# Late attention blocks: values two visits after their scores, an own buffer for transposed blocks, exponentials summed by ScalarE, and TensorE's order left free for longer

## The chip, the cores and the metric

The kernel runs on one core of one Trainium2 chip. The metric is the device time of one execution in microseconds (us); less is better. Before the change it took 1091.05 us, the median of three runs (1088.34, 1091.05 and 1091.76).

A core has several engines that run at the same time, each through its own fixed list of instructions: TensorE (PE in the profile; PEld is its loading of weights), VectorE (DVE), ScalarE (ACT), GpSimd (POOL) and SyncE (SP). SP and POOL here mostly issue DMA transfers, each from a queue of its own and in order. An instruction that must wait holds up everything behind it on its engine.

## The reference

Attention inside blocks of 64 tokens, and behind it a feed-forward layer with PReLU. Cut to what is computed:

```python
# q, k, v: (8, 8, 576, 64) float32; 9 chunks of 64 tokens in each (batch, head)
scores = (1 / sqrt(64)) * q_c @ k_c.transpose
scores = scores - max(scores, axis=-1, keepdims=True)
attn = exp(scores)
attn = attn / (sum(attn, axis=-1, keepdims=True) + 1e-09)
x = (attn @ v_c) laid out as 4608 tokens x 512

h = x @ w_in                              # 512 x 2048
g = maximum(h, 0) + alpha * minimum(h, 0)
out = g @ w_out                           # 2048 x 512
```

## The kernel before

**Tiling.** The 4608 tokens are 36 subtiles of 128 tokens (two chunks of 64, eight heads), and 9 blocks of 512 tokens (four subtiles). The width of 2048 is cut into 16 slices `f` of 128. Every matrix product of the feed-forward layer is done three times, with a high and a low part of each operand in float32r (high x high, high x low, low x high); `split_weight` (L119 to L138) makes the two parts of the weights on ScalarE and VectorE, 32 times, one tile `wi` and one tile `wo` for each `f`.

**Plain stage.** Blocks 0, 1 and 2 are multiplied as they stand. A step is one (block, `f`): `ffn_in` (L314 to L334; 12 matmuls of 128x512 in L320, then PReLU and the split of its result into `gh` and `gl`), and later `ffn_out` (L336 to L347; 12 matmuls in L344, which add to four banks `ps_o0` to `ps_o3`). There are 48 steps, n = 0 to 47, in five phases: block 0 with f 0 to 3, block 1 with f 0 to 8, block 0 with f 4 to 15, block 1 with f 9 to 15, block 2. The four banks serve one phase at a time: at its end `store` (L351 to L380) empties them. The first part of blocks 0 and 1 goes to DRAM, and at the end of the block's second phase it is read back and added on VectorE (L367) in a tile of the name `raw` or `t1`. The first matmul of the next phase's `ffn_out` into a bank waits until that bank has been read. The second half of a step follows its first half one step later while n < 4, and two steps later from there on (the list `pending`).

**Paired stage.** Blocks 3 to 8 go in three pairs, each by a scheme with seven products in place of eight. Each of the seven weights is a sum or difference of quarters of the weights. `combine(side, j)` (L478 to L507) makes them, 16 times: 8 VectorE operations, two ScalarE copies, two tiles `t1` (two buffers), two tiles `raw` (three buffers), and seven DMAs on POOL that write the results to DRAM (`keep_a`). They come back through SP's queue as a stream (L524) through five buffers. `first_product(j)` (L591 to L622, matmuls in L586), eight times in a pair, computes h and PReLU; `second_product` (L624 to L697, matmuls in L669) the rest. For it `operand` builds the seven operands: for operand 7 a difference on VectorE in a tile `t3` with one buffer (L633), another difference in place (L636), then `split` on ScalarE and VectorE (L542, L543). Every third operand splits into the two `t1` tiles, the others into `gh` and `gl`. `convert` (L545 to L569) does the same for x of the next pair, between.

**Attention.** Subtiles 0 to 7 are done early, with buffers of their own. Subtiles 8 to 35 are done in **visits** (L399 to L413). A visit takes two banks `ps_a` and does the values of an old subtile (32 matmuls of 64x64, L283) and the scores of a new one (32 matmuls, L196) on TensorE, then copies the old result into x (`attn_x`), does the softmax of the new one (`attn_softmax`: maxima L210, subtraction L216, one exponential over 128x512 on ScalarE L217, sums L226, reciprocal, scaling L229), and `attn_blocks`: VectorE transposes 32x32 blocks (L236) into a tile taken from the one buffer named `q_sb`, and eight DMAs on SP's queue (L243) move those blocks to `pT`, which the values read. The old subtile is always the one before the new. The loads of the next subtile (q into that same `q_sb`, k, v; L156, L158, L165) are called after the visit. Subtiles 8 to 20 are visited at the plain steps 23, 25, 27, 29, 31, 33, 34, 36, 37, 39, 40, 42, 43; the others ahead of each `first_product` of the first and second pair. The last pair has no visits.

**What sets the order.** A scheduler orders each engine's instructions by dependences, buffers and priorities; attention work, PReLU and the emptying of banks have high priority. TensorE's matmuls are kept in the order of the program from step 4 on (`pinned`, L710; `pe`, near L107). Combines come at every odd step from 15 on, one each.

Of the kernel before, what the change touches and what calls it, by code (L numbers as in the profile page):

```python
# [27 lines left out]
def tile_local_attention_prelu_ffn(  # L28
# [12 lines left out]
    nc = tc.nc  # L41
# [15 lines left out]
    JF = NF // 2  # L57
    EARLY = 2 * SPB

    BIASED = (6,) * SPB + (8,) * SPB  # L60
    TURNS = (4, 9)
    HIGH = 300

# [141 lines left out]
    def attn_softmax(s, sc3):  # L205
        early = s < EARLY
        mx = soft.tile([P, H, 1], F32, name="mx", bufs=2)
        parts = [(slice(0, H), sc3)] if early else [(slice(b * NP, (b + 1) * NP), sc3[b]) for b in range(2)]
        for g, part in parts:
            nc.vector.tensor_reduce(mx[:, g], part, axis=AX.X, op=ALU.max)  # L210
        pr = prs[s // 2 % 2][:, s % 2] if early else soft.tile([P, H, C], F32, name="pr")
        sm = soft.tile([P, H, 1], F32, name="sm", bufs=2)
        m = BIASED[s] if early else 0
        if not early:
            for g, part in parts:
                nc.vector.tensor_tensor(pr[:, g], part, mx[:, g].broadcast_to([P, NP, C]), op=ALU.subtract)  # L216
            nc.scalar.activation(pr, pr, AF.Exp, scale=SCALE)  # L217
        elif m < H:
            nc.vector.tensor_tensor(pr[:, m:], sc3[:, m:], mx[:, m:].broadcast_to([P, H - m, C]), op=ALU.subtract)
            nc.scalar.activation(pr[:, m:], pr[:, m:], AF.Exp, scale=SCALE)  # L220
        if m:
            nc.vector.tensor_scalar(mx[:, :m], mx[:, :m], -SCALE, None, op0=ALU.mult)
            for g in range(m):
                nc.scalar.activation(pr[:, g], sc3[:, g], AF.Exp, bias=mx[:, g], scale=SCALE, accum_out=sm[:, g])
        if m < H:
            nc.vector.tensor_reduce(sm[:, m:], pr[:, m:], axis=AX.X, op=ALU.add)  # L226
        nc.vector.tensor_scalar(sm, sm, 1e-9, None, op0=ALU.add)
        nc.vector.reciprocal(sm, sm)
        nc.vector.tensor_tensor(pr, pr, sm.broadcast_to([P, H, C]), op=ALU.mult)  # L229
        probs[s] = pr  # L230

    def attn_blocks(s):

        pr = probs.pop(s)
        tb = load.tile([P, 2, H, HALF], F32, name="q_sb")
        nc.vector.transpose(tb.rearrange("p j h t -> p h j t"), pr)  # L236
        pT = load.tile([P, 2, H, HALF], F32, name="pT")
        for c in range(2):
            for i in range(2):
                for j in range(2):  # L240
                    src = slice(c * C + i * HALF, c * C + (i + 1) * HALF)
                    dst = slice(c * C + j * HALF, c * C + (j + 1) * HALF)
                    nc.sync.dma_start(  # L243
                        out=pT[dst, i].rearrange("p h t -> p (h t)"),
                        in_=tb[src, j].rearrange("p h t -> p (h t)"),
                    )
        pdiag[s] = pT
# [151 lines left out]
    def visit(old, new):  # L399

        att[:] = [ps_a.tile([P, TB], F32, name="ps_a") for _ in range(2)]
        with tc.high_priority(offset=HIGH):
            if old is not None:
                xo = attn_values(old)
            if new is not None:
                sc3 = attn_scores(new)
            if old is not None:
                attn_x(old, xo)
            if new is not None:
                attn_softmax(new, sc3)  # L410
                attn_blocks(new)
        if new is not None and new + 1 < NSUB:
            attn_load(new + 1)  # L413

    attn_load(0, "q")
    fetch("wi", 0)
# [23 lines left out]
            if 0 <= i - st < SPB:  # L440
                beside[i * n0 // (SPB + 2)].append((st, SPB + i - st))

    visits = [2 * NF - 9 + 2 * j for j in range(SPB + 1)]
    visits += [2 * NF + 1 + 3 * j // 2 for j in range(2 * SPB)]
    late = {}
    for j, at in enumerate(visits):
        old, new = EARLY + j - 1, EARLY + j
        late[at] = (old if j else None, new)

    pending = []  # L450

# [172 lines left out]
    def second_product(g, b, conversion, end):  # L624
# [4 lines left out]
        def operand(i, j):  # L629
            b11, b12, b21, b22 = g[j][:, 0], g[j][:, 1], g[JF + j][:, 0], g[JF + j][:, 1]  # L630
            if i == 7:
                t = stage.tile([P, TB], F32, name="t3", bufs=1)
                nc.vector.tensor_tensor(t, b22, b12, op=ALU.subtract)  # L633
            elif i in (5, 6, 4):
                one, two = {5: (b12, b11), 6: (b22, b12), 4: (b21, b12)}[i]
# [1 line left out]
                t = b12  # L637
            else:
                t = {1: b11, 3: b22, 2: b21}[i]
            pool, names = (stage, ("t1", "t1")) if count[0] % 3 == 2 else (gp, ("gh", "gl"))  # L640
            count[0] += 1
            hi, lo = (pool.tile([P, TB], F32R, name=name) for name in names)
            split(t, hi, lo)
# [61 lines left out]
    for n, (p, b, f) in enumerate(steps):  # L705
# [4 lines left out]
                x[b + 1] = new_x()  # L710
        if n == 2 * NF:
            new_raw(PLAIN)
        pinned[0] = n >= n0
        for st, s in beside[n]:
            attend(st, s)
        if n in late:
            if late[n][0] is None:
                attn_load(late[n][1])
            visit(*late[n])
        if ready < NF:  # L720
            prepare(ready)
            ready += 1
        elif n % 2 and combined:
            combine(*combined.pop(0))
        if n == len(steps) - 3:
            ops, conversion = convert(PLAIN)
# [3 lines left out]
                    conversion.pop(0)()  # L730
        pending.append((acc, ffn_in(x[b], f), f, f0, f1, b, False))

        if len(pending) > (1 if n < n0 else 2):
            second(*pending.pop(0))
    assert not combined and not conversion
    for _ in range(3):
# [6 lines left out]
    for pair in range(NPAIR):  # L743
# [5 lines left out]
        for j in range(JF):  # L749
            if more:  # L750
                new += 1
                visit(new - 1, new if new < NSUB else None)
            first_product(ops, g, j)
        if more:
            ops, conversion = convert(b + 2)
# [40 lines left out]
```

## Time and profile before

| | value |
|---|---|
| median of 3 runs | 1091.05 us |
| the profiled execution's own time | 1095.3 us |
| its span, first to last instruction | 1093.5 us |
| TensorE busy, matmuls / weight loads | 893.8 us (82%) / 695.3 us |
| VectorE busy | 745.1 us (68%) |
| ScalarE busy | 494.6 us (45%) |
| GpSimd busy | 115.5 us (11%) |
| mean granted TensorE clock | 0.897 |
| moved by DMA | 184.51 MB, 169 GB/s |
| chain that ended last, shares | PE 50%, DVE 18%, DMA 16%, SP's queue 7%, waiting for nothing shown 5%, ACT 3% |

How to read the rows: engines are PE, PEld, DVE, ACT, POOL, SP; a name with q is that engine's DMA queue. `L320` is line 320 of the kernel. `out<-in` names the tiles, `x24` counts. A row of the waits gives the waiting engine, tile and line, then what released it, the summed wait in us, how often, and the mean. A row of the timeline gives the start in us from the span's start, the duration, engine, line, operation and, in brackets, the idle time before it with its releaser. A row of the page's 40 slices has one digit for each slice of 27.3 us: the busy share, or the granted clock, in tenths.

### The profile page before, as it was taken

Reading aid. Unit: us, or ns where it says so; the run is one execution under the profiler, and the core shown is the slowest. Engines: PE = TensorE matmul, PEld = TensorE weight load, DVE = VectorE, ACT = ScalarE, POOL = GpSimd, SP = SyncE. Lnnn points to the kernel's source line nnn. Section 1 sums busy time; section 2 is a strip of 40 time slices with the busy share of each in tenths; the row PEclk is TensorE's granted clock in tenths of the full one; section 3 lists DMA queues with packets and bytes.
Section 4 is the critical chain, followed back from the end, with each engine's and each line's share of the span. In section 5 each row is a group of like instructions: output and inputs, shape, how many; then the busy total and the mean of one; then the engine's idle time right before and its main releaser. Section 6 shows DMA issues by size and latency. Waiting matters only on the chain.

```text
span 1093.5 us, 14954 instructions
## 1 busy us (share of the span) xinstructions
PE 893.8 (82%) x5248; PEld 695.3 (64%) x5248; DVE 745.1 (68%) x1369; ACT 494.6 (45%) x946; POOL 115.5 (11%) x174
## 2 busy tenths in 40 slices
PE   4889999766755688967685899787786999998998
PEld 3568887545544567756563577665664778886676
DVE  6799998865684346545457876555559784657875
ACT  6666565423232234433345454334355543665543
POOL 4023232423042000000000001000000001000000
PEclk9889999887876888978888899988897999999999
DMA  9557673565456221454545357645442567554464
GB/s 281 171 182 245 213 255 128 193 196 175 136 186 213 65 59 51 145 164 142 165 146 165 96 192 217 217 131 196 129 160 86 165 193 250 193 183 163 154 194 153
DMA packets 69211, 184.51 MB, mean 169 GB/s; under 512 B 11408, under 2 KB 18576, under 8 KB 69136
## 3 DMA queue, kind: packets, MB, share of 16 engines
q1 hardware_dynamic: 56672, 143.17, 42.1%
q0 software_dynamic: 12320, 40.38, 10.2%
q8 instruction: 42, 0.69, 0.3%
q14 instruction: 33, 0.27, 0.1%
q10 hardware_dynamic: 144, 0.01, 0.0%
HBM read 135.27 MB, written 40.89 MB: 161 GB/s over the span
## 4 chain that ended last, share of the span: by engine, by line
PE 50%; DVE 18%; DMA 16%; SPq 7%; issue 5%; ACT 3%; POOL 0%; DVEq 0%; ACTq 0%; POOLq 0%
PE ps_o L669 12%; PE ps_o L586 9%; PE ps_h L320 8%; DMA q_sb<-qT 8%; PE ps_o L344 8%; SPq L243 7%; PE ps_h L669 6%; PE ps_h L586 4%; DMA pT<-q_sb 3%; PE ps_a L196 2%; DMA wi<-kT 2%; DVE t L633 1%; DMA wo_a<-raw 1%; DVE q_sb L236 1%; DVE gl L543 1%
## 5 line engine op out<-in xcount | busy, mean ns | idle before, releaser
L344 PE MATMUL ps_o<-wo,gh 128*128 128x512 f32 x384 | 119.7, 395 | 1.4 <-DVE raw L367 1.4
L320 PE MATMUL ps_h<-xh,wi 128*128 128x512 f32 x384 | 119.1, 437 | 0.8 <-ACT xh L301 0.8
L586 PE MATMUL ps_o<-wi,raw 128*128 128x512 f32 x222 | 96.1, 433 | 0.0
L196 PE MATMUL ps_a<-k_sb,q_sb 64*64 64x64 f32 x896 | 28.7, 295 | 82.1 <-DMA q_sb<-qT 82.1
L210 DVE TENSOR_REDUCE mx<-ps_a 128x4 f32<-128x256 f32 (+1 forms) x64 | 26.9, 450 | 100.8 <-ACT xl L297 52.1
L586 PE MATMUL ps_o<-wo,raw 128*128 128x512 f32 x222 | 94.1, 424 | 0.0
L320 PEld LDWEIGHTS ps_h<-xh,wi 128*128 128x128 f32 x384 | 78.9, 211 | 21.5 <-ACT xh L301 1.2
L344 PEld LDWEIGHTS ps_o<-wo,gh 128*128 128x128 f32 x384 | 72.1, 188 | 19.3 <-DVE raw L367 1.8
L196 PEld LDWEIGHTS ps_a<-k_sb,q_sb 64*64 64x64 f32 x896 | 23.9, 198 | 86.4 <-DMA q_sb<-qT 85.9
L283 PE MATMUL ps_a<-pT,v_sb 64*64 64x64 f32 x896 | 29.4, 252 | 57.4 <-DMA pT<-q_sb 44.3
L344 PE MATMUL ps_o<-wo,gl 128*128 128x512 f32 x192 | 74.9, 395 | 0.0
L283 PEld LDWEIGHTS ps_a<-pT,v_sb 64*64 64x64 f32 x896 | 23.2, 158 | 70.2 <-issue 63.0
L669 PE MATMUL ps_o<-gh,raw 128*128 128x512 f32 x188 | 64.7, 396 | 0.9 <-ACT gh L542 0.8
L658 POOL DMA_DIRECT2D outT<-xl x10 | 5.4, 540 | 555.4 <-DVE xl L648 555.2
L542 ACT CAST gh<-wi 128x512 fp32r<-128x512 f32 x63 | 39.3, 624 | 48.8 <-PE ps_o L669 28.1
L320 PE MATMUL ps_h<-xl,wi 128*128 128x512 f32 x192 | 60.0, 440 | 0.0
L543 DVE TENSOR_TENSOR gl<-wi,gh 128x512 fp32r<-128x512 f32 x63 | 43.3, 688 | 22.7 <-ACT gh L542 22.3
L310 ACT ACTIVATE g<-ps_h 128x512 f32<-128x512 f32 x48 | 28.7, 599 | 66.3 <-PE ps_h L320 66.3
L586 PEld LDWEIGHTS ps_o<-wi,raw 128*128 128x128 f32 x222 | 46.3, 209 | 11.9
L586 PEld LDWEIGHTS ps_o<-wo,raw 128*128 128x128 f32 x222 | 46.2, 208 | 11.0
L320 PEld LDWEIGHTS ps_h<-xl,wi 128*128 128x128 f32 x192 | 42.1, 219 | 10.8
L312 DVE SCALAR_TENSOR_TENSOR g<-ps_h,g 128x512 f32<-128x512 f32 x48 | 32.8, 684 | 19.2 <-ACT g L311 19.1
(245 smaller groups left out, 2199.1 us busy)
## 6 DMA issues: line engine op xcount, KB each, us to landing
raw<-wi_a SPq DMA_DIRECT2D x51, 512.0 KB, 3.9
raw<-wo_a SPq DMA_DIRECT2D x51, 512.0 KB, 3.4
wi<-wi_a SPq DMA_DIRECT2D x17, 512.0 KB, 3.5
wo<-wo_a SPq DMA_DIRECT2D x17, 512.0 KB, 3.4
raw<-w_in SPq DMA_DIRECT2D x16, 512.0 KB, 4.4
raw<-w_out SPq DMA_DIRECT2D x16, 512.0 KB, 4.0
wi_a<-raw POOLq DMA_DIRECT2D x32, 256.0 KB, 3.6
wo_a<-raw POOLq DMA_DIRECT2D x32, 256.0 KB, 3.7
```

Of the source, the lines that this page charges most:

```text
L196: pe(nc.tensor.matmul(att[par][c * C:(c + 1) * C, (NP + hp) * C:(NP + hp + 1) * C], lhsT=q_sb[rows, 2 * hp + c], rhs=kb[rows, 2 * hp + c], ...
L210: nc.vector.tensor_reduce(mx[:, g], part, axis=AX.X, op=ALU.max)
L243: nc.sync.dma_start(out=pT[dst, i].rearrange("p h t -> p (h t)"), in_=tb[src, j].rearrange("p h t -> p (h t)"),)
L283: pe(nc.tensor.matmul(att[c][par * C:(par + 1) * C, hp * C:(hp + 1) * C], lhsT=v_sb[rows, h * C:(h + 1) * C], rhs=p[rows, :, par * NP + hp ...
L310: nc.scalar.activation(g, h, AF.Relu, scale=-1.0)
L312: nc.vector.scalar_tensor_tensor(g, in0=h, scalar=0.0, in1=g, op0=ALU.max, op1=ALU.subtract)
L320: pe(nc.tensor.matmul(hps, lhsT=wi[f][:, l, k * P:(k + 1) * P], rhs=xx[:, k], start=(i == 0 and k == 0), stop=(i == 2 and k == NK - 1),))
L344: pe(nc.tensor.matmul(o, lhsT=a[:, ts], rhs=wo[f][:, l], start=(f == first and i == 0), stop=(f == last and i == 2),))
L542: nc.scalar.copy(t_hi, t)
L543: nc.vector.tensor_tensor(t_lo, t, f32(t_hi), op=ALU.subtract)
L586: pe(nc.tensor.matmul(ps, lhsT=w[:, l, k * P:(k + 1) * P], rhs=xx[:, xl], start=first and at == 0, stop=at == n - 1, skip_group_check=not ...
L669: pe(nc.tensor.matmul(ps[m], lhsT=w[:, l, m * P:(m + 1) * P], rhs=xx, start=i != 6 and j == 0 and n == 0, stop=j == JF - 1 and n == 2, ski ...
```

## The change

The lines of the changed kernel are 4 lower than before between about L234 and L400, and 7 lower from about L412 on (L367 is now L363, L524 is now L517).

- **Values two visits later.** A visit's old subtile is the new one less two. `pT` has two buffers. In the paired stage the two visits after the last scores have values alone, so of the 16 visits there, 14 bring scores; the plain stage's visits take one more subtile, 8 to 21, at other steps.
- **Own buffer.** The transposed blocks go to the tile `t3` of one buffer, not to `q_sb`. The second product's operand 7, which used `t3`, takes a tile `g` (two buffers), and another operand in three splits into `t1`.
- **Loads.** The next subtile's q and k and this subtile's v are called inside the visit, right after its scores.
- **Exponentials.** In late subtiles, too, each head has an exponential of its own on ScalarE, with the negated maximum as bias, which also returns its row sums; the subtraction (L216) and the sums (L226) on VectorE go.
- **Order.** TensorE's order is kept from step 20 on, not from step 4, and the second halves follow one step behind until step 19.
- **Combines** come at every step up to 24, and at every odd step after it.

```diff
@@ -57,7 +57,7 @@
     JF = NF // 2
     EARLY = 2 * SPB
 
-    BIASED = (6,) * SPB + (8,) * SPB
+    BIASED = (6,) * SPB + (8,) * (NSUB - SPB)
     TURNS = (4, 9)
     HIGH = 300
 
@@ -205,23 +205,19 @@
     def attn_softmax(s, sc3):
         early = s < EARLY
         mx = soft.tile([P, H, 1], F32, name="mx", bufs=2)
-        parts = [(slice(0, H), sc3)] if early else [(slice(b * NP, (b + 1) * NP), sc3[b]) for b in range(2)]
-        for g, part in parts:
-            nc.vector.tensor_reduce(mx[:, g], part, axis=AX.X, op=ALU.max)
         pr = prs[s // 2 % 2][:, s % 2] if early else soft.tile([P, H, C], F32, name="pr")
         sm = soft.tile([P, H, 1], F32, name="sm", bufs=2)
-        m = BIASED[s] if early else 0
-        if not early:
-            for g, part in parts:
-                nc.vector.tensor_tensor(pr[:, g], part, mx[:, g].broadcast_to([P, NP, C]), op=ALU.subtract)
-            nc.scalar.activation(pr, pr, AF.Exp, scale=SCALE)
-        elif m < H:
+        m = BIASED[s]
+        parts = [(slice(0, H), sc3)] if early else [(slice(b * NP, (b + 1) * NP), sc3[b]) for b in range(2)]
+        for at, part in parts:
+            nc.vector.tensor_reduce(mx[:, at], part, axis=AX.X, op=ALU.max)
+        if m < H:
             nc.vector.tensor_tensor(pr[:, m:], sc3[:, m:], mx[:, m:].broadcast_to([P, H - m, C]), op=ALU.subtract)
             nc.scalar.activation(pr[:, m:], pr[:, m:], AF.Exp, scale=SCALE)
-        if m:
-            nc.vector.tensor_scalar(mx[:, :m], mx[:, :m], -SCALE, None, op0=ALU.mult)
-            for g in range(m):
-                nc.scalar.activation(pr[:, g], sc3[:, g], AF.Exp, bias=mx[:, g], scale=SCALE, accum_out=sm[:, g])
+        nc.vector.tensor_scalar(mx[:, :m], mx[:, :m], -SCALE, None, op0=ALU.mult)
+        for g in range(m):
+            one = sc3[:, g] if early else sc3[g // NP][:, g % NP]
+            nc.scalar.activation(pr[:, g], one, AF.Exp, bias=mx[:, g], scale=SCALE, accum_out=sm[:, g])
         if m < H:
             nc.vector.tensor_reduce(sm[:, m:], pr[:, m:], axis=AX.X, op=ALU.add)
         nc.vector.tensor_scalar(sm, sm, 1e-9, None, op0=ALU.add)
@@ -232,9 +228,9 @@
     def attn_blocks(s):
 
         pr = probs.pop(s)
-        tb = load.tile([P, 2, H, HALF], F32, name="q_sb")
+        tb = stage.tile([P, 2, H, HALF], F32, name="t3", bufs=1)
         nc.vector.transpose(tb.rearrange("p j h t -> p h j t"), pr)
-        pT = load.tile([P, 2, H, HALF], F32, name="pT")
+        pT = load.tile([P, 2, H, HALF], F32, name="pT", bufs=2)
         for c in range(2):
             for i in range(2):
                 for j in range(2):
@@ -404,13 +400,14 @@
                 xo = attn_values(old)
             if new is not None:
                 sc3 = attn_scores(new)
+                if new + 1 < NSUB:
+                    attn_load(new + 1, "q")
+                attn_load(new, "v")
             if old is not None:
                 attn_x(old, xo)
             if new is not None:
                 attn_softmax(new, sc3)
                 attn_blocks(new)
-        if new is not None and new + 1 < NSUB:
-            attn_load(new + 1)
 
     attn_load(0, "q")
     fetch("wi", 0)
@@ -440,12 +437,8 @@
             if 0 <= i - st < SPB:
                 beside[i * n0 // (SPB + 2)].append((st, SPB + i - st))
 
-    visits = [2 * NF - 9 + 2 * j for j in range(SPB + 1)]
-    visits += [2 * NF + 1 + 3 * j // 2 for j in range(2 * SPB)]
-    late = {}
-    for j, at in enumerate(visits):
-        old, new = EARLY + j - 1, EARLY + j
-        late[at] = (old if j else None, new)
+    visits = [21, 23, 25, 27, 29, 30, 33, 35, 36, 38, 39, 41, 42, 44]
+    late = {at: (EARLY + j - 2 if j > 1 else None, EARLY + j) for j, at in enumerate(visits)}
 
     pending = []
 
@@ -629,7 +622,7 @@
         def operand(i, j):
             b11, b12, b21, b22 = g[j][:, 0], g[j][:, 1], g[JF + j][:, 0], g[JF + j][:, 1]
             if i == 7:
-                t = stage.tile([P, TB], F32, name="t3", bufs=1)
+                t = gp.tile([P, TB], F32, name="g")
                 nc.vector.tensor_tensor(t, b22, b12, op=ALU.subtract)
             elif i in (5, 6, 4):
                 one, two = {5: (b12, b11), 6: (b22, b12), 4: (b21, b12)}[i]
@@ -637,7 +630,7 @@
                 t = b12
             else:
                 t = {1: b11, 3: b22, 2: b21}[i]
-            pool, names = (stage, ("t1", "t1")) if count[0] % 3 == 2 else (gp, ("gh", "gl"))
+            pool, names = (stage, ("t1", "t1")) if count[0] % 3 == 0 else (gp, ("gh", "gl"))
             count[0] += 1
             hi, lo = (pool.tile([P, TB], F32R, name=name) for name in names)
             split(t, hi, lo)
@@ -710,17 +703,17 @@
                 x[b + 1] = new_x()
         if n == 2 * NF:
             new_raw(PLAIN)
-        pinned[0] = n >= n0
+        pinned[0] = n >= 20
         for st, s in beside[n]:
             attend(st, s)
         if n in late:
-            if late[n][0] is None:
-                attn_load(late[n][1])
+            if n == visits[0]:
+                attn_load(late[n][1], "q")
             visit(*late[n])
         if ready < NF:
             prepare(ready)
             ready += 1
-        elif n % 2 and combined:
+        elif (n < 25 or n % 2) and combined:
             combine(*combined.pop(0))
         if n == len(steps) - 3:
             ops, conversion = convert(PLAIN)
@@ -730,7 +723,7 @@
                     conversion.pop(0)()
         pending.append((acc, ffn_in(x[b], f), f, f0, f1, b, False))
 
-        if len(pending) > (1 if n < n0 else 2):
+        if len(pending) > (1 if n < 20 else 2):
             second(*pending.pop(0))
     assert not combined and not conversion
     for _ in range(3):
@@ -749,7 +742,7 @@
         for j in range(JF):
             if more:
                 new += 1
-                visit(new - 1, new if new < NSUB else None)
+                visit(new - 2, new if new < NSUB else None)
             first_product(ops, g, j)
         if more:
             ops, conversion = convert(b + 2)
```

Three places where instructions now stand in another order. First, SP's queue, which issues its DMAs in this order, at one visit in the first product of the first pair. `pT` are the copies of transposed blocks, `q_sb`, `k_sb`, `v_sb` the loads of one subtile, and `wi_a` the stream of combined weights. Before:

```order
L524 DMA wi15_4146<-wi_a8_368 128x1024
L243 DMA pT_4121<-q_sb_4119 32x256 x8
L524 DMA wo15_4163<-wi_a9_369 128x1024
L524 DMA raw_4191<-wi_a10_370 128x1024
L156 DMA q_sb_4130<-qT 128x512
L524 DMA raw_4282<-wi_a11_371 128x1024
L165 DMA v_sb_4276<-v 128x512
L158 DMA k_sb_4273<-kT 128x512
```

The same stretch of SP's queue in the changed kernel:

```order
L239 DMA pT_4105<-t3_4103 32x256 x8
L156 DMA q_sb_4225<-qT 128x512
L158 DMA k_sb_4226<-kT 128x512
L165 DMA v_sb_4229<-v 128x512
L517 DMA raw_4180<-wi_a7_367 128x1024
L517 DMA wi15_4271<-wi_a8_368 128x1024
L517 DMA wo15_4288<-wi_a9_369 128x1024
L517 DMA raw_4316<-wi_a10_370 128x1024
L239 DMA pT_4252<-t3_4250 32x256 x8
```

Before, the q load stood behind the copies that read its buffer and behind two pieces of the weight stream; now the three loads stand ahead of the stream and ahead of their own visit's copies.

Second, VectorE at the end of block 0's second phase, where `store` adds the two partial sums (`ps_o0` to `ps_o3` are the four banks). Before:

```order
L500 TENSOR_TENSOR t1_2077<-t1_2077 128x256
L505 TENSOR_TENSOR raw_2087<-t1_2077,raw_2087 128x512
L505 TENSOR_TENSOR raw_2092<-t1_2079,raw_2092 128x512
L367 TENSOR_TENSOR raw_2163<-ps_o0_1557,raw_2163 128x512
L367 TENSOR_TENSOR t1_2171<-ps_o2_1559,t1_2171 128x512
L367 TENSOR_TENSOR t1_2175<-ps_o3_1560,t1_2175 128x512
L307 TENSOR_TENSOR xl_2008<-ps_a_2179,xh_2007 128x4x64
...
L229 TENSOR_TENSOR pr_2220<-pr_2220,sm_2221 128x512
L367 TENSOR_TENSOR raw_2167<-ps_o1_1558,raw_2167 128x512
L236 STREAM_TRANSPOSE q_sb_2229<-pr_2220 128x8x2x32
```

VectorE at the same store in the changed kernel (L480 to L498 are a combine, L363 is the addition):

```order
L498 TENSOR_TENSOR raw_2124<-t1_2114,raw_2124 128x512
L498 TENSOR_TENSOR raw_2129<-t1_2116,raw_2129 128x512
L480 TENSOR_TENSOR t1_2242<-wo2_580 128x512
L480 TENSOR_TENSOR t1_2244<-wo10_1163 128x512
...
L498 TENSOR_TENSOR raw_2252<-t1_2242,raw_2252 128x512
L498 TENSOR_TENSOR raw_2257<-t1_2244,raw_2257 128x512
L363 TENSOR_TENSOR t1_2336<-ps_o2_1517,t1_2336 128x512
L363 TENSOR_TENSOR t1_2340<-ps_o3_1518,t1_2340 128x512
L363 TENSOR_TENSOR raw_2328<-ps_o0_1515,raw_2328 128x512
L363 TENSOR_TENSOR raw_2332<-ps_o1_1516,raw_2332 128x512
```

Before, six combines stood ahead of this store on VectorE and a visit between its third and fourth addition; now eleven combines stand ahead of it and the four additions follow each other. Ahead of block 1's store it was ten, and is now fifteen.

Third, VectorE at the end of the first pair's first product in the changed kernel, from the last visit's maxima (L213) to the end of the second product's eighth operand (the last row here, a split in L536):

```order
L213 TENSOR_REDUCE mx_5121<-ps_a_5079 128x4
L213 TENSOR_REDUCE mx_5121<-ps_a_5080 128x4
L217 TENSOR_SCALAR mx_5121<-mx_5121 128x8
L595 TENSOR_TENSOR gh_5167<-ps_h_5150,gh_5167 128x512
L626 TENSOR_TENSOR g_5230<-wo7_4152,wi7_4151 128x512
...
L626 TENSOR_TENSOR g_5340<-wo14_5189,wi14_5188 128x512
L536 TENSOR_TENSOR wo5_5538<-xl_4043,wo5_5538 128x512
L629 TENSOR_TENSOR wi14_5188<-wi14_5188 128x512
L536 TENSOR_TENSOR gl_5343<-g_5340,gh_5342 128x512
```

From the first of these rows to the last it is 62 instructions. The first difference for operand 7 (L626) now stands inside the last visit, ahead of its transpose; before, it stood in `t3` and could not be followed by another until the split had read it.

## The prediction

> **What bounds the kernel now.** I read the page first, then TensorE's waits, one visit in the timeline, and busy times by stage.
>
> ```profile
> span 1093.5 us, 14954 instructions
> ...
> PE   4889999766755688967685899787786999998998
> ...
> PEclk9889999887876888978888899988897999999999
> ```
>
> TensorE is the engine to follow, but it isn't full everywhere: from slice 8 to 31 (each 27.3 us) most stand at 5 to 8 tenths, and its granted clock sinks there too. What it waits for:
>
> ```profile
> PE ps_a L196 <- DMA q_sb<-qT: 82.1, 24, 5.6
> PE ps_a L283 <- DMA pT<-q_sb: 44.3, 22, 6.1
> ...
> PE ps_a L283 <- DVE t L497: 8.8, 2, 6.3
> ```
>
> 135 us, all in the late visits. One of them, in the timeline:
>
> ```profile
> 458.52 4.94 SPq L243 DMA_DIRECT2D pT<-q_sb  x8
> ...
> 464.87 1.12 PE L283 MATMUL ps_a<-pT,v_sb 64*64 64x64 f32 x30 [0.81 <-DMA pT<-q_sb]
> ...
> 464.91 0.34 SPq L156 DMA_DIRECT2D q_sb<-qT  x1
> ...
> 469.69 1.13 PE L196 MATMUL ps_a<-k_sb,q_sb 64*64 64x64 f32 x32 [3.70 <-DMA q_sb<-qT]
> ...
> 471.77 0.63 PE L586 MATMUL ps_h<-wi,wi 128*128 128x512 f32 x1
> ...
> 472.19 0.63 PE L586 MATMUL ps_h<-wo,wi 128*128 128x512 f32 x1
> ```
>
> The q load goes out only at 464.91, when the eight copies that read the same q_sb buffer have landed; the scores behind it start at 469.69. Values wait for the copies, scores for the load, and afterwards matmuls start 0.42 us apart for a while. By stage (engine columns: busy us of PE, PEld, DVE, ACT, POOL; then granted clock, DMA share, GB/s):
>
> ```profile
> 180.40:235.20 54.80, 38.49 (x284) 29.89 (x282) 41.80 (x89) 20.64 (x36) 19.02 (x27) 0.81 0.60 197
> 235.20:451.20 216.00, 155.58 (x1157) 122.65 (x1157) 123.52 (x244) 71.65 (x127) 32.56 (x47) 0.82 0.39 121
> 451.20:592.00 140.80, 106.98 (x849) 84.56 (x849) 79.61 (x149) 56.69 (x104) 1.30 (x3) 0.84 0.52 166
> 592.00:622.40 30.40, 17.93 (x50) 10.92 (x50) 29.56 (x48) 14.49 (x26) 0.00 (x0) 0.78 0.31 99
> ...
> 691.70:825.50 133.80, 103.44 (x757) 81.28 (x753) 75.81 (x139) 56.33 (x104) 0.53 (x1) 0.86 0.51 164
> 825.50:854.90 29.40, 17.88 (x49) 10.68 (x49) 28.92 (x47) 14.07 (x26) 0.00 (x0) 0.77 0.23 72
> ...
> 923.30:1001.50 78.20, 78.20 (x337) 62.92 (x336) 47.14 (x73) 44.41 (x78) 1.08 (x2) 1.00 0.60 194
> 1001.50:1021.20 19.70, 15.08 (x49) 8.38 (x48) 19.15 (x30) 8.09 (x15) 0.00 (x0) 1.00 0.35 111
> ```
>
> The last pair's first product (923.3) has no visits: 336 matmuls in 78.2 us, 0.233 us each at clock 1.00. The same work with visits took 140.8 and 133.8 us. After each first product comes a stretch (592.0, 825.5, 1001.5) in which VectorE is full and TensorE waits: the first eight operands of the second product.
>
> **The change, part by part.** A visit's own work on TensorE is what it took where nothing was late:
>
> ```profile
> 451.18 0.69 PE L283 MATMUL ps_a<-pT,v_sb 64*64 64x64 f32 x32
> ...
> 452.27 0.51 PE L586 MATMUL ps_o<-wi,raw 128*128 128x512 f32 x1
> ```
>
> 1.1 us.
>
> *Values two visits later, own buffer, earlier loads.* A visit's copies now have a whole further visit to land, some 22 us in a first product against about 13 from maxima to landing (452.8 to 466). The q load has no copies before it in its buffer; it waits only for the scores that read it, and has 9.8 us of products for its 4.5 us (464.91 to 469.69 with k and the start). I cost both waits at nothing. Their cover is the next 9.8 us of products, or 5.6 us of one step where two visits follow at once; without it a visit costs the 4 to 7 us of now.
>
> - Plain stage from 235.2 to 451.2. Left on TensorE: 20 first and 23 second halves of steps, 12 matmuls each, 43 x 12 x 0.233 = 120 us, 10 visits 11 us: 131. With a slow restart and small holds at the second store I take 138 instead of 216: **-78** (bounds -60, at 156, TensorE's busy time now; -84, at 132).
> - Pair 0, 451.2 to 622.4 = 171.2 us. The last visit ends 7 x 9.8 + 8 x 1.1 = 77 us in, some 3 us more with lag; from there the changed order has 62 VectorE instructions to the eighth operand, most of them of 512 columns, which start 0.60 us apart where VectorE is full:
>
> ```profile
> 825.58 0.68 DVE L543 TENSOR_TENSOR wo<-xl,wo 128x512 fp32r<-128x512 f32 x1
> 826.18 0.68 DVE L560 TENSOR_TENSOR g<-xl 128x512 f32<-128x512 f32 x1
> ```
>
>   so 36 us, and 1.4 for its six matmuls: 118, taken as 119, **-52** (bounds -40, -58).
> - Pair 1, 691.7 to 854.9 = 163.2 us: two visits without scores, about 53 such instructions after the last: 115, **-48** (-36, -54).
> - Last pair's stretch: operand 7 gets a two-buffer tile for a one-buffer one, and about 15 VectorE instructions stand behind the last PReLU in place of 20: **-4** (0, -7). The t1 tiles' new turn I cost at nothing.
>
> *Exponentials summed by ScalarE.* The operations that go, and eight exponentials with sums as they ran early, up to the next instruction:
>
> ```profile
> L217 ACT ACTIVATE pr<-pr 128x512 f32<-128x512 f32 x28 | 17.6, 630 | 33.7 <-DVE pr L216 33.6
> ...
> L216 DVE TENSOR_TENSOR pr<-ps_a,mx 128x256 f32<-128x256 f32 x56 | 21.0, 413 | 0.0
> ...
> L226 DVE TENSOR_REDUCE sm<-pr 128x8 f32<-128x512 f32 x28 | 19.1, 684 | 15.1 <-ACT pr L217 15.1
> ...
> 67.15 0.31 ACT L224 ACTIVATE wi<-ps_a,mx 128x64 f32<-128x64 f32 x1
> ...
> 69.48 0.63 ACT L301 CAST xh<-ps_a 128x512 fp32r<-128x512 f32 x1
> ```
>
> ScalarE: 2.33 for 0.63, +1.7 us a visit, 48 us in all; VectorE: -(21.0 + 19.1)/28 plus a small scaling, -1.25 us, -35 in all. Neither is TensorE's path by itself. In a first product ScalarE then has about 44.4/8 + 0.7 + 2.3 = 8.6 us of work in a 10.9 us period, VectorE 47.1/8 + 2.7 = 8.6. The loop through both (exponentials, normalising, t, PReLU, next visit's copies behind it) I work out at about 12 us from these durations: 1 us a period of lag, which is the 3 us above; unabsorbed it is a rival.
> [...]
>
> *TensorE's order free through step 19.* Up to 180 us TensorE hardly waits, so I give it 0 (-5 to +5).
>
> *Combines moved forward.* This is the part that costs. Block 0's stored sums (L367) free the four banks for the next phase, and need the raw and t1 buffers that combines hold:
>
> ```profile
> 177.25 0.69 DVE L137 SCALAR_TENSOR_TENSOR wo<-t,t 128x512 fp32r<-128x512 uint32 x1
> ...
> 220.04 1.29 DVE L505 TENSOR_TENSOR raw<-t,raw 128x512 fp32r<-128x512 f32 x2 [0.68 <-ACT raw L504]
> ...
> 234.45 0.69 DVE L367 TENSOR_TENSOR raw<-ps_o,raw 128x512 f32<-128x512 f32 x1
> ...
> 235.19 0.73 PE L344 MATMUL ps_o<-wo,gh 128*128 128x512 f32 x2 [1.38 <-DVE raw L367]
> ...
> 323.04 1.28 DVE L505 TENSOR_TENSOR raw<-t,raw 128x512 fp32r<-128x512 f32 x2
> ...
> 328.19 1.37 DVE L505 TENSOR_TENSOR raw<-t,raw 128x512 fp32r<-128x512 f32 x2 [0.22 <-ACT raw L504]
> ```
>
> After the last weight is split (177.25) six combines stand ahead of that store now, eleven afterwards, and two more visits. Five at 5.15 us (323.04 to 328.19) are 26, two visits' VectorE work 6; the visit that now sits inside the store (5 us) moves ahead of it. So the store ends 27 us later, near 262, and TensorE, with 32 us of work after 180, stands still from about 211. Queued behind the held matmuls is all of TensorE's order, and with it every later visit. **+27** (bounds: +14, if VectorE's 13 us of idle time in 180.4 to 235.2 take up part; +40, at the 7.3 us that the six combines took on average between 177 and 221).
>
> **Sum**, against the profiled execution, 1095.3 us (span 1093.5 and 1.8 around it): 27 - 78 - 52 - 48 - 4 = -155, so 940. The median shown is 1091.05, 4 lower: **936**.
>
> **Rivals.**
> 1. *The store is hardly late*: VectorE's idle time absorbs the combines. For it: 41.8 busy of 54.8 us. Against: six combines in a row with three raw buffers. About +5 to +14 in place of 27: 905 to 923, say 914.
> 2. *ScalarE and VectorE become the bound*: the 12 us loop sets the period of 14 loaded visits and the lag isn't absorbed, and the close visits of the plain stage lose 1 us each: +15 to +45, 966. For it: 8.6 of 10.9 us on both. Against: TensorE has five of its six banks to work in while one waits to be emptied.
> 3. *A transfer takes the place of the wait*: 140.8 us x 166 GB/s in 89 us is 263 GB/s, near the most this trace shows (281 in the first slice), and SP's queue is in order, so a q load can sit behind eight copies (4.94 us) that wait for a transpose. Half the 127 us of q and pT waits would stay: 1000.
> 4. *Slower: the clock.* TensorE's work at full clock is about 3168 x 0.233 = 738 us plus 35 of small matmuls. If the denser run were granted less for good, it costs 773 x (1/c - 1): at the 0.81 of the 180.4 row, +181, 1117; slower from c = 0.83 on. Against: 1.00 from 854.9 to 1001.5 at full load; the low grants stand only beside waits. [...]
>
> **Chances.** Forecast 0.47 (920 to 958); rival 1 0.19; rival 2 0.20; rival 3 0.10; rival 4 0.03; the change doing next to nothing 0.01. Less than 0.3% can't be told from no change. Faster 0.96, same 0.01, slower 0.03. The bounds added up: 40 - 60 - 40 - 36 - 0 = -96, so 995, and 14 - 84 - 58 - 54 - 7 = -189, so 902. I give **902 to 995**: it holds nearly all of the forecast and of rivals 1 and 2, and leaves out rivals 3 and 4 and what lies beyond the bounds, some 2 in 10.
>
> **What would show it.** Waits of L196 for q_sb and of L283 for pT near nothing; one hold of about 50 us before a second half of a step near 211 to 262, released by the store's addition; from there steps at 5.6 us; first products of about 90 us at clock 1.00; the three stretches behind them still full of VectorE. I am wrong if TensorE waits for copies or loads at visits, if the hold is missing or over 70 us, or if first products take over 100 us.

## The result, and the profile after

The changed kernel takes **938.77 us** (median of 4 runs, 937.79 to 939.85); before it is 1090.46 in the same comparison. The ratio is 0.8611, 95% interval 0.8591 to 0.863. The page of the changed kernel, its span, TensorE's busy tenths and its granted clock in 40 slices (now of 23.4 us):

```profile
span 935.6 us, 15350 instructions
...
PE   4798999990399999999886999999879999998998
...
PEclk9999999995599999999996999999969999999999
```

TensorE is at 9 nearly everywhere. What is left are one hole of two slices (the tenth and eleventh digit, 210 to 257 us) and the two dips behind the first products. TensorE's waits of the changed kernel (engine, tile and line, releaser; us in total, times, longest: the last number of such a row is the longest wait, here and in the rows ahead, where it was called the mean):

```profile
PE ps_o L340 <- DVE raw L363: 41.3, 2, 39.4
...
PE ps_a L196 <- DMA k_sb<-kT: 1.7, 1, 1.7
```

Of the 126 us at the q loads and the copies nothing is left in this view; one wait of 39.4 us for the store of block 0 has come, the hold that the prediction put between 211 and 262 us. By stage (columns as before):

```profile
180.00:247.80 67.80, 28.41 (x268) 22.43 (x261) 57.98 (x119) 28.58 (x87) 33.01 (x46) 0.74 0.70 232
247.80:392.65 144.85, 139.32 (x1156) 110.03 (x1156) 90.65 (x183) 82.91 (x267) 18.67 (x28) 0.96 0.46 146
392.65:485.70 93.05, 90.43 (x849) 71.67 (x848) 64.82 (x127) 67.48 (x222) 1.33 (x3) 0.98 0.72 239
485.70:516.30 30.60, 18.15 (x49) 11.81 (x49) 30.60 (x52) 16.19 (x29) 0.00 (x0) 0.72 0.40 135
584.07:673.38 89.31, 87.89 (x786) 69.88 (x785) 62.33 (x118) 63.27 (x191) 1.08 (x2) 1.00 0.70 236
673.38:701.71 28.33, 18.35 (x49) 11.77 (x48) 28.33 (x48) 15.53 (x28) 0.00 (x0) 0.70 0.24 76
769.50:847.90 78.40, 78.40 (x338) 63.08 (x337) 48.11 (x75) 43.98 (x77) 1.08 (x2) 1.00 0.58 195
847.90:863.81 15.91, 11.91 (x49) 8.78 (x48) 15.76 (x27) 8.41 (x16) 0.00 (x0) 1.00 0.41 133
```

The first products with visits take 93.1 and 89.3 us in place of 140.8 and 133.8, at a clock of 0.98 and 1.00. The stretches behind them are as long as before (30.6 and 28.3 us), VectorE is full in them. Against the profile of before, from span to span (1093.5 to 935.6, -157.9). The 235.2 of before is where the matmuls of the store's second bank begin, behind the fourth addition; the same matmuls begin at 251.4 in the changed kernel, and the first row goes by them. The row of pair 1 begins at the first matmul of its first product (691.7 and 585.15).

| stage | before, us | change forecast | change measured |
|---|---|---|---|
| up to the second bank behind block 0's store | 235.2 | +27 | +16.2 |
| from there to the first pair | 216.0 | -78 | -74.7 |
| pair 0 to its eighth operand | 171.2 | -52 | -47.5 |
| pair 1, the same | 163.2 | -48 | -46.6 |
| last pair's first eight operands | 19.7 | -4 | -3.8 |
| all the rest | | 0 | -1.5 |

One visit of the changed kernel, in the timeline (start, duration, engine or queue, line):

```profile
404.23 0.65 PE L196 MATMUL ps_a<-k_sb,q_sb 64*64 64x64 f32 x32
406.26 1.26 SPq L156 DMA_DIRECT2D q_sb<-qT  x1
...
413.00 6.32 SPq L239 DMA_DIRECT2D pT<-t  x8
...
414.80 0.69 PE L279 MATMUL ps_a<-pT,v_sb 64*64 64x64 f32 x32
...
415.31 0.65 PE L196 MATMUL ps_a<-k_sb,q_sb 64*64 64x64 f32 x32
```

The next subtile's q goes out 2 us after the scores, and the next scores start 11.1 us after these, although this visit's copies are still being issued (413.00 to 419.32): the values at 414.80 read those of the visit before. The whole chain from scores to issued copies, 15 us, is longer than the period; it now merely overlaps it.

The hold, on VectorE and TensorE of the changed kernel:

```profile
240.15 1.37 DVE L498 TENSOR_TENSOR raw<-t,raw 128x512 fp32r<-128x512 f32 x2 [0.27 <-ACT raw L497]
243.53 0.69 DVE L363 TENSOR_TENSOR t<-ps_o,t 128x512 f32<-128x512 f32 x1 [2.01 <-DMA t<-partial]
...
246.97 0.69 DVE L363 TENSOR_TENSOR raw<-ps_o,raw 128x512 f32<-128x512 f32 x1 [1.02 <-DMA raw<-partial]
...
247.81 1.19 PE L340 MATMUL ps_o<-wo,gh 128*128 128x512 f32 x2 [39.39 <-DVE raw L363]
...
250.64 0.69 DVE L363 TENSOR_TENSOR raw<-ps_o,raw 128x512 f32<-128x512 f32 x1 [2.98 <-DMA raw<-partial]
...
251.38 1.22 PE L340 MATMUL ps_o<-wo,gh 128*128 128x512 f32 x2 [1.95 <-DVE raw L363]
```

The eleventh combine ends at 241.5, the additions that free the banks follow, and TensorE restarts, with the first bank at 247.81 and with the second at 251.38. Between the combine and the fourth addition the chain that ended last has two transfers (start, duration): the combine's result on its way to DRAM, and then the stored sum that is read back.

```profile
241.86 4.80 DMA wo_a<-raw
246.73 3.79 DMA raw<-partial
```

The additions of before, between the two that the prediction shows, and the matmuls of the first bank, in the kernel before:

```profile
223.66 0.69 DVE L367 TENSOR_TENSOR raw<-ps_o,raw 128x512 f32<-128x512 f32 x1 [2.33 <-DMA raw<-partial]
228.70 1.29 DVE L367 TENSOR_TENSOR t<-ps_o,t 128x512 f32<-128x512 f32 x2 [4.35 <-DMA t<-partial]
...
232.94 0.63 PE L344 MATMUL ps_o<-wo,gh 128*128 128x512 f32 x2
```

There the sixth combine ended at 221.3, and the second bank's matmuls began 13.9 us later: the stored sums were read back late, and a visit stood ahead of the fourth addition. The first bank did not wait for the store at all.

### The profile page after: what moved, and what is told of

It reads as the page before. It is cut to its first block, busy times and chain, and to the rows that moved or that the text cites. A ratio compares the mean times of both kernels' runs of the same rounds, so it can differ in the third digit from the quotient of the medians.

```text
span 935.6 us, 15350 instructions
## 1 busy us (share of the span) xinstructions
PE 830.7 (89%) x5248; PEld 653.4 (70%) x5248; DVE 703.7 (75%) x1313; ACT 540.1 (58%) x1366; POOL 115.2 (12%) x174
## 4 chain that ended last, share of the span: by engine, by line
PE 68%; DVE 15%; DMA 9%; ACT 3%; SPq 2%; issue 2%; POOL 0%; DVEq 0%; ACTq 0%
PE ps_o L662 15%; PE ps_o L579 14%; PE ps_h L316 11%; PE ps_o L340 11%; PE ps_h L579 7%; PE ps_h L662 7%; DMA wi<-kT 2%; DMA raw<-wi_a 2%; PE ps_a L279 1%; DVE g L626 1%; DVE wi L629 1%; SPq L239 1%; DVE gl L536 1%; DMA wi<-wi_a 1%; DVE raw L498 1%
## 5 line engine op out<-in xcount | busy, mean ns | idle before, releaser
L316 PE MATMUL ps_h<-xh,wi 128*128 128x512 f32 x384 | 108.0, 404 | 1.3 <-DVE g L308 1.3
L579 PE MATMUL ps_o<-wi,raw 128*128 128x512 f32 x222 | 89.4, 403 | 2.3 <-DMA raw<-wi_a 2.3
L316 PEld LDWEIGHTS ps_h<-xh,wi 128*128 128x128 f32 x384 | 71.6, 190 | 19.4 <-DVE g L308 1.8
L220 ACT ACTIVATE pr<-ps_a,mx 128x64 f32<-128x64 f32 x224 | 67.0, 327 | 13.0 <-DVE mx L217 13.0
L662 PE MATMUL ps_o<-gh,raw 128*128 128x512 f32 x184 | 61.5, 393 | 0.0
L536 DVE TENSOR_TENSOR gl<-wi,gh 128x512 fp32r<-128x512 f32 x63 | 42.8, 688 | 18.4 <-ACT gh L535 18.2
L316 PE MATMUL ps_h<-xl,wi 128*128 128x512 f32 x192 | 53.8, 400 | 0.0
L220 ACT ACTIVATION_READ_ACCUMULATOR pr<-ps_a,mx 128x1 f32 x224 | 49.2, 219 | 0.0
L306 ACT ACTIVATE wo<-gh 128x512 f32<-128x512 f32 x24 | 15.2, 634 | 54.5 <-DVE gh L602 54.5
L328 ACT CAST gh<-g 128x512 fp32r<-128x512 f32 x48 | 29.8, 621 | 28.9 <-DVE g L308 17.2
L497 ACT CAST raw<-t 128x512 fp32r<-128x512 f32 x32 | 19.2, 625 | 42.8 <-DVE t L492 28.0
L662 PE MATMUL ps_o<-gl,raw 128*128 128x512 f32 x92 | 36.8, 400 | 6.9 <-DVE gl L536 6.9
```

What stands on the lines that cost most here:

```text
L220: nc.scalar.activation(pr[:, g], one, AF.Exp, bias=mx[:, g], scale=SCALE, accum_out=sm[:, g])
L306: nc.scalar.activation(g, h, AF.Relu, scale=-1.0)
L316: pe(nc.tensor.matmul(hps, lhsT=wi[f][:, l, k * P:(k + 1) * P], rhs=xx[:, k], start=(i == 0 and k == 0), stop=(i == 2 and k == NK - 1),))
L328: nc.scalar.copy(gh, g)
L497: nc.scalar.copy(w[:, 0], t)
L536: nc.vector.tensor_tensor(t_lo, t, f32(t_hi), op=ALU.subtract)
```

## The experiments

All start from the changed kernel; each ratio is to the kernel before, with its 95% interval. The changed kernel stands at 0.8611 (0.8591 to 0.863).

### e1_pace: combines at the pace of before

```diff
-        elif (n < 25 or n % 2) and combined:
+        elif n % 2 and combined:
```

> The changed kernel with combines at odd steps only, as before: 6 combines stand ahead of block 0's store on VectorE in place of 11, and 10 in place of 15 ahead of block 1's. Theory (the hold of 39.4 us before the second half of a step is made of the combines ahead of the store): five combines of about 4.7 us (227.46 to 232.15 to 236.75 us in the changed kernel) go from it, 23 us, so TensorE restarts near 225 us in place of 247.8; the combines come back on VectorE between later visits, where VectorE is idle 4 tenths of the time, for 0 to 6 us: 916 to 923 us. Rival 1 (what the combines save later is worth as much as the hold costs, since they sit between softmax and PReLU in the plain stage): the hold shrinks, but later steps take longer than 5.6 us, 932 to 945. Rival 2 (the hold is set by reading the stored sums back, 1 to 3 us for each of four): 936 to 940.

Measured: **920.60 us**, 0.8433 (0.8392 to 0.8475). The end of the sixth combine, TensorE's restart with the first and the second bank, and a visit's copies and a read-back on SP's queue, in this run:

```profile
220.87 0.65 DVE L498 TENSOR_TENSOR raw<-t,raw 128x512 fp32r<-128x512 f32 x1
...
221.61 6.83 SPq L239 DMA_DIRECT2D pT<-t  x8
...
225.82 1.19 PE L340 MATMUL ps_o<-wo,gh 128*128 128x512 f32 x2 [13.17 <-DVE raw L363]
...
228.69 0.38 SPq L362 DMA_DIRECT2D raw<-partial  x1
...
232.16 1.22 PE L340 MATMUL ps_o<-wo,gh 128*128 128x512 f32 x2 [4.72 <-DVE raw L363]
```

The wait falls from 39.4 to 13.2 us and the first bank's restart comes 22.0 us earlier; the second bank's, at 232.2 in place of 251.4, comes 19.2 us earlier, and 18 us reach the end. So the theory holds, and moving the combines forward made the changed kernel slower. Six combines end at 221.5, as they did before (221.3), so the five others cost 20 us here (241.5), 4 each. The second wait, 4.7 us, is not made of combines: the second bank's stored sum is read back only at 228.7, behind the eight copies of a visit in SP's queue, a part of rival 2.

### e2_onevisit, e3_shared, e6_both: the delay and the buffer apart

e2_onevisit takes the delay away:

```diff
-    visits = [21, 23, 25, 27, 29, 30, 33, 35, 36, 38, 39, 41, 42, 44]
-    late = {at: (EARLY + j - 2 if j > 1 else None, EARLY + j) for j, at in enumerate(visits)}
+    visits = [23, 25, 27, 29, 30, 33, 35, 36, 38, 39, 41, 42, 44]
+    late = {at: (EARLY + j - 1 if j else None, EARLY + j) for j, at in enumerate(visits)}
...
-                visit(new - 2, new if new < NSUB else None)
+                visit(new - 1, new if new < NSUB else None)
```

> The changed kernel with values one visit after their scores again (13 visits in the plain stage, 16 in the pairs, 15 of them with scores); own buffer, loads inside the visit and all else stay. Theory (the delay is what hides the copies): in the changed kernel the copies land some 16 us after their scores (404.2 to about 420.5), and a visit's period in a first product is 11.1, so the values and the scores queued behind them come every 16 to 17 us: +40 to +45 in each of the pairs, +35 to +50 in the plain stage: 1050 to 1075. Rival (the q loads were the larger wait, 82.1 of 135 us before, and the own buffer alone takes it away): half of the gain stays, 1000 to 1025.

e3_shared takes the own buffer and the early loads away (the same loads are issued behind `attn_blocks`), and e6_both both:

```diff
-        tb = stage.tile([P, 2, H, HALF], F32, name="t3", bufs=1)
+        tb = load.tile([P, 2, H, HALF], F32, name="q_sb")
```

> The changed kernel with the transposed blocks in q's buffer again and the loads after the visit; values stay two visits later. Theory (the q load must wait until the eight copies have landed, so the chain from scores over copies and load to the next scores stays whole, and the delay of the values alone gives nothing): a visit's period in a first product is again 17 to 20 us, 1065 to 1110. Rival (the waits add up, and only the 82 us at the scores come back): 1015 to 1035.

> Both undone together: values one visit after their scores, transposed blocks in q's buffer and loads after the visit; exponentials, combines and TensorE's order stay as changed. Theory (behind a shared buffer the chain from scores over copies and load to the next scores sets the period, and values that come with it cost nothing more): the same as with the shared buffer alone, 1085 to 1110. Rival (the two effects add): 88 us above that run, 1170 to 1190.

Measured:

| | own buffer, loads inside the visit | q's buffer, loads after the visit |
|---|---|---|
| values two visits later | 938.77, the changed kernel | 1096.59 (e3_shared), 1.0071 (1.0045 to 1.0097) |
| values one visit later | 1026.78 (e2_onevisit), 0.9404 (0.9358 to 0.9451) | 1100.62 (e6_both), 1.0128 (1.0081 to 1.0175) |

The delay alone brings 4 us and can't be told from none, the buffer with its loads alone 74, both together 162. The buffer and the place of the loads were not taken apart. One visit of e3_shared in the timeline, and its largest wait:

```profile
483.01 1.13 PE L196 MATMUL ps_a<-k_sb,q_sb 64*64 64x64 f32 x32 [6.74 <-DMA q_sb<-qT]
...
490.02 4.95 SPq L239 DMA_DIRECT2D pT<-q_sb  x8
...
496.33 0.33 SPq L156 DMA_DIRECT2D q_sb<-qT  x1
...
501.52 1.13 PE L196 MATMUL ps_a<-k_sb,q_sb 64*64 64x64 f32 x32 [4.63 <-DMA q_sb<-qT]
```

```profile
PE ps_a L196 <- DMA q_sb<-qT: 141.0, 23, 15.2
```

Scores, copies, load, scores are one ring of 18.5 us here, and of 18.3 to 19.5 us in the same product of e6_both, with the values inside it; the waits at the values have moved to the scores. So the 82.1 and 44.3 us of before were not two independent waits but two places on one ring: with the buffer shared, taking the values out of it brings nothing that can be told. With the own buffer but without the delay (e2_onevisit) the ring is scores, copies, values:

```profile
486.27 1.16 PE L196 MATMUL ps_a<-k_sb,q_sb 64*64 64x64 f32 x31
...
493.28 4.95 SPq L239 DMA_DIRECT2D pT<-t  x8
...
499.62 0.63 PE L279 MATMUL ps_a<-pT,v_sb 64*64 64x64 f32 x27 [1.43 <-DMA pT<-t]
...
500.09 0.68 PE L196 MATMUL ps_a<-k_sb,q_sb 64*64 64x64 f32 x31
```

13.8 us here, 14.7 on the mean over the first product (471.06 to 544.53 us, five periods). I had expected 16 to 17 from the changed kernel, where the copies take 6.32 us to be issued; here it is 4.95, which is 1.4 us of the difference. The plain stage loses what the theory says (the first pair begins at 442.2 in place of 392.7, 49.6 us later); the pairs, to the eighth operand, lose 18.6 and 24.1 us where 40 to 45 were expected. So this run lies below its theory and 2 us above the rival's range, though the ring is the theory's.

### e4_oneexp: the late softmax of before

```diff
-        m = BIASED[s]
+        m = BIASED[s] if early else 0
...
+        if not early:
+            for at, part in parts:
+                nc.vector.tensor_tensor(pr[:, at], part, mx[:, at].broadcast_to([P, NP, C]), op=ALU.subtract)
+            nc.scalar.activation(pr, pr, AF.Exp, scale=SCALE)
```

> The changed kernel with the late softmax of before: subtraction on VectorE, one exponential of 128x512, sums on VectorE. Theory (neither engine is TensorE's path by itself; VectorE has 1.25 us more a visit, ScalarE 1.7 less, and only the visits inside the hold and at the end of each first product count): three visits in the hold and one at the end of each of two products, +2 to +8: 940 to 947. Rival 1 (ScalarE decides in the visits, so one exponential is better): 925 to 935. Rival 2 (VectorE decides all through the visits, 28 x 1.25 us): 960 to 975.

Measured: 942.27 us, 0.863 (0.859 to 0.8671): inside the theory's range and not to be told from the changed kernel. TensorE's restart in this run:

```profile
253.14 1.19 PE L344 MATMUL ps_o<-wo,gh 128*128 128x512 f32 x2 [43.58 <-DVE raw L367]
```

5.3 us later than in the changed kernel, since VectorE has more to do where it is late (63.1 us busy from 180 us to the restart, against 58.0); the two pairs, to the eighth operand, are 3.7 and 1.8 us shorter. It comes out even.

### e5_pinned: TensorE's order kept from step 4

```diff
-        pinned[0] = n >= 20
+        pinned[0] = n >= n0
...
-        if len(pending) > (1 if n < 20 else 2):
+        if len(pending) > (1 if n < n0 else 2):
```

> The changed kernel with TensorE's order kept, and second halves two steps behind, from step 4 on, as before. Theory (TensorE runs out of work at 208.3 us and stands for 39.4 us until VectorE has done the combines and the store, so what it gains ahead of that it loses in the wait): the wait shrinks by what TensorE is late, 936 to 942 us. Rival (the free order feeds VectorE and ScalarE earlier and so brings the store forward): 945 to 960.

Measured: 939.81 us, 0.8639 (0.8609 to 0.8669): no difference, as the theory has it. The restart is at 251.4, 3.6 us later, and is made up for by the end.

### e8_t3: operand 7 in the one-buffer tile

```diff
-                t = gp.tile([P, TB], F32, name="g")
+                t = stage.tile([P, TB], F32, name="t3", bufs=1)
...
-            pool, names = (stage, ("t1", "t1")) if count[0] % 3 == 0 else (gp, ("gh", "gl"))
+            pool, names = (stage, ("t1", "t1")) if count[0] % 3 == 2 else (gp, ("gh", "gl"))
```

> The changed kernel with operand 7 in the one-buffer tile t3 and every third operand's turn as before (t3 is also the visits' transposed blocks). Theory: the last pair's first eight operands take 19.7 us again in place of 15.9, +4, and the two other pairs, where the operands begin inside the last visits, +0 to +3 each: 941 to 949. Rival (TensorE gets the same operands no later, since VectorE is full there in both): 936 to 941.

Measured: 951.28 us, 0.8738 (0.8698 to 0.8779), 12.5 us slower than the changed kernel and 2 above the theory's range. The last pair's eight operands take 19.6 us (852.6 to 872.2), +3.7 as expected. Pair 0, from its first product to the eighth operand, takes 4.9 us longer, and at the end of that first product stands a wait that the changed kernel hasn't:

```profile
484.96 5.58 SPq L239 DMA_DIRECT2D pT<-t  x8
...
494.44 0.68 DVE L626 TENSOR_TENSOR t<-wo,wi 128x512 f32<-128x512 f32 x1
495.83 0.80 PE L662 MATMUL ps_o<-gh,wi 128*128 128x512 f32 x1 [10.57 <-ACT gh L535]
```

The first operand's difference (L626) writes `t3`, so on VectorE it stands behind the last visit's transpose into that tile and the copies that read it, at 494.4; in the changed kernel it stands ahead of that transpose, at 479.9. VectorE is full up to it (no idle time from 481.8 us on), and TensorE waits 10.6 us for this operand. So the new tile for operand 7 is what the own buffer of the blocks requires.

### e7_pace2, e9_mixed, e10_later: what is left of the hold

```diff
+    TIMES = (15, 17, 19, 21, 27, 29, 31, 35, 36, 37, 38, 39, 40, 41, 43, 45)
...
-        elif (n < 25 or n % 2) and combined:
+        elif n in TIMES and combined:
```

e9_mixed adds the old softmax for subtiles 22 to 35; e10_later besides it begins TIMES with 19, 21, 27, 28, 29, 30, 31 in place of its first seven numbers.

> The changed kernel with combines at steps 15, 17, 19, 21, 27, 29, 31, each from 35 to 41, 43 and 45: four ahead of block 0's store and seven ahead of block 1's. Theory (the 13.2 us that TensorE still waited with six, and 4.7 us at the second store, are combines): two fewer at 4.7 us take 9 us from the first wait and the second goes, and two or three steps with a combine each give some back: 906 to 914. Rival (the combines from 35 on, one each step of 5.6 us with visits beside, fill VectorE and hold PReLU): 920 to 935.

> As e7_pace2, but subtiles 22 to 35, which are visited in the pairs, have the softmax of before (one exponential, subtraction and sums on VectorE). Theory (e4_oneexp was the same in all because one exponential cost 5.3 us at block 0's store, 253.1 us in place of 247.8, and gave back 3.7 and 1.7 us in the two pairs, from the first product's start to the eighth operand): without the loss at the store the gain in the pairs stays, 5 us below e7_pace2: 904 to 909. Rival (the pairs of e4_oneexp were shorter only because they began later): 910 to 914.

> As e9_mixed, with combines at steps 19, 21, each from 27 to 31, each from 35 to 41, 43 and 45: two ahead of block 0's store, still seven ahead of block 1's. Theory (the 8.1 us that TensorE still waits at block 0's store are the last two of four combines, at 4.4 us): the wait goes, 6 to 8 us below e9_mixed: 897 to 902. Rival (five combines in a row of five steps, with visits beside, make VectorE late at block 1's store or hold PReLU): 904 to 912.

Measured: 911.86 us, 0.8377 (0.8349 to 0.8406); 908.30 us, 0.8333 (0.8294 to 0.8372); **901.23 us**, 0.8266 (0.823 to 0.8302). With four combines ahead of the store TensorE still waits 8.1 us, in e7_pace2:

```profile
205.28 1.25 DVE L499 TENSOR_TENSOR raw<-t,raw 128x512 fp32r<-128x512 f32 x2
...
205.75 0.33 SPq L362 DMA_DIRECT2D raw<-partial  x1
206.17 5.83 SPq L239 DMA_DIRECT2D pT<-t  x8
...
213.88 0.33 SPq L362 DMA_DIRECT2D raw<-partial  x1
...
219.10 1.22 PE L340 MATMUL ps_o<-wo,gh 128*128 128x512 f32 x2 [8.12 <-DVE raw L363]
```

The last combine ends here at 206.5, and the second bank's stored sum goes out only at 213.9, behind a visit's eight copies and three loads in SP's queue. So these 8.1 us are a read-back, as the 4.7 us of e1_pace were (they lie at this store too, not at the second one), and not the combines that the theories of e7_pace2 and e10_later counted there. With two combines, in e10_later, all four read-backs (189.1 to 200.5) go out ahead of the next copies (202.7). TensorE's largest wait from 180 to 400 us is then this, and its only one for a store, which is block 1's, the second row:

```profile
PE ps_a L284 <- ACT pr L225: 7.8, 7, 1.8
...
PE ps_o L345 <- DVE t L368: 0.8, 1, 0.8
```

Both times come out as expected, and the waits for block 0's store are gone. But behind the large hold, which is VectorE full of combines, lay a smaller one in the order of SP's queue; that fewer combines are what moved the read-backs forward is not shown apart. What is left at the visits are short waits for ScalarE, rival 2 of the prediction on a small scale.

e9_mixed lies inside its range, but not by its theory: pair 0 takes 122.2 us from its first product's first matmul to its eighth operand against 122.4 in e7_pace2, pair 1 114.8 against 116.3, and the intervals of the two runs overlap. The 3.7 us of e4_oneexp in pair 0 did not return; what made them is open. e10_later beats both kernels, by 17% and 4%.

## Why the prediction was right

- **The waits of the visits go (-78, -52, -48 forecast; -74.7, -47.5, -46.6 measured).** The mechanism is shown by the four corners of the table above: the copies have to be off TensorE's ring and the load out of their buffer, and one without the other gives less than half, or nothing. The sizes were somewhat too large. In the plain stage I allowed 7 us beyond TensorE's bare 131, and it is 10.3: the first nine matmuls of it took 4.0 us (251.38 to 255.39) where 2.1 is their full pace, and a load of k (1.7 us) and ScalarE's exponentials (1.7) still held visits. In pair 0 the last visit ended 83.2 us in (forecast 80): pieces of the weight stream were 2.6 us late behind the copies in SP's queue, a small form of rival 3.
- **The hold by the combines (+27 forecast, +16.2 measured)** lies inside its bounds, near the lower one (+14). Place and mechanism were right, and the size was wrong in one step. "Five at 5.15 us are 26, two visits' VectorE work 6": all of it together moved the last combine by 20.2 us (221.3 to 241.5), which fits the idle time of VectorE in rival 1 (41.8 us busy of 54.8 before, 55.9 of 61.5 from 180 to 241.5 now). The other step came out: with "the visit that now sits inside the store (5 us)" gone, 13.9 us behind the last combine became 9.9. Most of these 9.9 are the two transfers shown above, so the buffers that combines hold delay the store as the prediction has it. e1_pace shows the hold by the number of combines alone; in e7_pace2 and e10_later the order of SP's queue changed with it.
- **Exponentials and free order, both at nothing:** e4_oneexp and e5_pinned show no difference. ScalarE's eight took 2.33 us (408.11 to 410.44), the price taken from the early ones.
- **Operand 7 (-4):** -3.8, and e8_t3 gives +3.7 back. That it was also needed by the own buffer, I had not said.
- **Rivals.** The lag of rival 2 did not come: periods in the first product are 11.1 us, of which the visit takes 1.1 and the products 10.0 (403.71, 404.80 and 414.80), up to the late pieces of the stream. Rival 4 did not come: the clock is 0.98 and 1.00 in the denser products.

The median lies 2.8 us above the forecast and the span's change 2.9 us below it (-157.9 for -155), but terms missed by more: the hold was 11 us less, the gains 9 us less (3 in the plain stage, 6 in the pairs), and 1.5 us came from elsewhere. They cancelled, so the closeness of the total is in part luck.

## What to carry to other kernels

Waits that a profile lists under two tiles may be one ring: write down what each step waits for all the way round, and count the ring's length against the time of the work that could hide it; an edit that leaves the ring whole gains nothing (the delay alone), one that shortens it gains in part (the buffer alone, 74 us), and only both together took it off TensorE's path (162). When TensorE becomes faster, look for the next engine that feeds its banks: here work without a deadline (the combines) stood ahead of a store with one, and moving it by a few steps was worth 27 us more (e7_pace2). Then look at the queue behind it: what was left of the hold was a read-back that stood behind copies.

## What the runs showed of the hardware

Eight copies of 32 KB occupy SP's queue for 4.94 to 6.25 us before and for 4.94 to 8.69 us in the changed kernel: in the visit shown, a chain of 15 us, their issue (6.32 us) is the longest single part, and loads, pieces of the stream and read-backs behind them go out later; in e1_pace a read-back went out at 228.7 us, behind copies issued from 221.6 us on for 6.83 us. In pair 0's stretch of the changed kernel, behind waits of 2.0 to 3.4 us, TensorE's matmuls started 0.43 us apart from 497.57 to 499.28 us, against 0.23 at full pace, with 0.72 as the stretch's mean clock.
